# Chunked attention and a squared-ReLU FFN on one core: V of the first 512 tokens loaded in 1 KB packets and spread by TensorE

## The chip, the core and the metric

The kernel runs on one core of a Trainium2 chip. The metric is the device time of one execution in microseconds. Before the change three runs took 282.87, 282.85 and 281.72 us, so the median is 282.85 us. One further execution was taken by the hardware profiler. All trace times below are microseconds from the start of that execution's span.

## The reference

```python
# q, k, v: [8 batches, 8 heads, 576 tokens, 64], float32; attention inside chunks of 64 tokens
scores = matmul(q_c, k_c.T) / sqrt(64)           # per batch, head and chunk: 64 x 64
attn = exp(scores - max); attn = attn / sum(attn)
out = matmul(attn, v_c)
x = out.transpose(0, 2, 1, 3).reshape(4608, 512)  # tokens x (heads * 64)
h = maximum(x @ w_in, 0)                          # w_in 512 x 2048
y = (h * h) @ w_out                               # w_out 2048 x 512; y is 4608 x 512, float32
```

## The kernel before

The 4608 tokens are cut into 18 groups of 256, and two groups make a block of 512 tokens. For every block the kernel computes attention, then the first product of the FFN (`ffn_in`, matmuls at L479), then the second product. TensorE does the products of block j while the attention of later groups is put between them at slots that are written out by hand. The order of instructions on each engine is the order of the program text (`manual_schedule`), so a waiting instruction holds up everything behind it on its engine.

The first block has nothing in front of it. It has a path of its own, written at the end of the function, and this path is what the change touches. It works on halves of four heads (`u` = 0 and 1):

- `load_half` (L227) brings q and k of four heads and 512 tokens in one DMA on SP's queue. Four neighbouring tokens go to one partition, so the pieces are 1 KB long: partition p holds tokens 4p to 4p + 3. `load_v_half` (L236) brings V with one token to a partition in pieces of 256 B: four DMAs of 128 tokens for each half, into `v_first`, which lies in the buffer `w_sum` that is free until later. All these DMAs stand on SP's queue in the order q0, k0, q1, k1, eight of V, and then the weights (`load_w_in`, L162).
- `load_w_in(0, n_cast=2)` brings the first 256 of w_in's 2048 columns; POOL casts them to bf16 in two pieces (L165). One piece serves one `ft` of `ffn_in`.
- `transpose_half` (matmuls against the identity at L257, copies at L266) makes the transposed q and k of one half. For q the copy keeps the order of the PSUM bank; for k `by_token=True` puts the tokens back in order.
- `scores_half` (L278) makes the scores of one half, and ScalarE writes their exponentials `e` (L285).
- `values_half` (L298) multiplies `e` with V, which has a column of ones beside it; VectorE takes the reciprocal of that column (L305) and multiplies (L306).
- `transpose_x_half` (L314) transposes the result, and a copy (L318) puts it into `xT`. `ffn_in` reads `xT`: the steps `dt` = 0 and 1 read the heads of `u` = 0, the steps `dt` = 2 and 3 those of `u` = 1.
- `keep_busy(n)` (L325) is n matmuls of the identity whose result nobody reads.

`ps_ffn` is a ring of four PSUM banks, and `ps_att` a ring of two double banks. Each call takes the next buffer of its ring and waits until the last reader of that buffer is done. The opening ends with four steps of `ffn_in` for `ft` = 0 and 1 (those with `dt` = 0 and 1), the last `transpose_x_half` and its copy. From there on the main run of L479 goes through.

Of the kernel before, what the change touches and what calls it, by code (L numbers as in the profile page):

```python
# [10 lines left out]
FP32 = mybir.dt.float32  # L11
BF16 = mybir.dt.bfloat16
# [5 lines left out]
def kernel(  # L18
# [9 lines left out]
    nc = tc.nc  # L28

    B, H, S, D = q.shape  # L30
# [27 lines left out]
    const_pool = ctx.enter_context(tc.tile_pool(name="const", bufs=1))  # L58
# [5 lines left out]
    ps_ffn = ctx.enter_context(tc.tile_pool(name="ps_ffn", bufs=4, space=bass.MemoryType.PSUM))  # L64
# [6 lines left out]
    ident = const_pool.tile([128, 128], BF16, name="ident")  # L71
# [4 lines left out]
    w_sum = w_pool.tile([128, 3, n_ft // 2, d_model // 2], BF16, name="w_sum")  # L76
# [124 lines left out]
    def transpose_qk(g, q_pool, k_pool):  # L201
# [13 lines left out]
            transpose_paired(g, which, bank)  # L215
            copy_paired(copy, qkT[:, which], bank)

    v_first = w_sum.rearrange("p i f c -> p (i f c)")[:, 0:8 * H * (D + 1)].bitcast(
        FP32).rearrange("p (t h d) -> p t h d", t=4, h=H)
# [12 lines left out]

    def load_v_half(u):
        b, s = first
        for t in range(4):
            nc.sync.dma_start(  # L236
                out=v_first[:, t, 4 * u:4 * u + 4, 0:D],
                in_=v[b, 4 * u:4 * u + 4, s + 128 * t:s + 128 * t + 128, :].rearrange(
                    "h s d -> s h d"))

    def bank_bf16():
        return ps_ffn.tile([128, 512], FP32, name="ps_ffn").bitcast(BF16)

    def transpose_half(src, dst, copies, by_token=False):
        flat = dst.rearrange("c t h q -> c (t h q)")
        n = 1024 // len(copies)
        if len(copies) == 1:
            banks = [bank_bf16()] * 2
            at0 = (0, 512)
        else:  # L250
            banks = [bank_bf16(), bank_bf16()]
            at0 = (0, 0)
        for h in range(2):
            cols = banks[h][:, at0[h]:at0[h] + 512].rearrange("c (n i p) -> c i n p", n=8, i=4)
            for i in range(4):
                for a in range(2):
                    nc.tensor.transpose(  # L257
                        out=cols[64 * a:64 * a + 64, i],
                        in_=src[:, 2 * h + a, i, 1::2],
                        identity=ident)  # L260
        for i, copy in enumerate(copies):
            out_, in_ = flat[:, i * n:(i + 1) * n], banks[i][:, 0:n]
            if by_token:
                out_ = out_.rearrange("c (n p i) -> c n p i", n=8, i=4)
                in_ = in_.rearrange("c (n i p) -> c n p i", n=8, i=4)
            copy(out=out_, in_=in_)  # L266

    def scores_half(qkT):
        qT, kT = (qkT[:, w].rearrange("c t h q -> c (t h q)").rearrange(
            "c (h n q) -> c h n q", h=2, n=8) for w in range(2))  # L270
        ps = ps_att.tile([128, 1024], FP32, name="ps_att")
        for h in range(2):
            for t in range(4):
                for a in range(2):
                    for p in range(2):
                        rows = slice(64 * a, 64 * a + 64)
                        o0 = a * 512 + h * 256 + t * 64
                        nc.tensor.matmul(  # L278
                            out=ps[64 * p:64 * p + 64, o0:o0 + 64],
                            lhsT=kT[rows, h, 2 * t + p],  # L280
                            rhs=qT[rows, h, 2 * t + p],
                            start=True, stop=True)
        e = att_pool.tile([128, 2, n_hp, 2, 64], BF16, name="e")
        flat = e.rearrange("p a h t q -> p (a h t q)")
        nc.scalar.activation(  # L285
            out=flat.rearrange("p (b q i) -> p b q i", q=16, i=4),
            in_=ps.rearrange("p (b i q) -> p b q i", i=4, q=16), func=AF.Exp, scale=scale)
        return flat.rearrange("p (a h t q) -> p a h t q", a=2, h=2, t=4)

    def values_half(e, x, u, j):  # L290
        v_bf = v_first.bitcast(BF16)
        ps = ps_att.tile([128, 2, 512], FP32, name="ps_att")
        for t in range(2):
            for h in range(2):
                for a in range(2):
                    for p in range(2):
                        o0 = (2 * t + h) * (D + 1)
                        nc.tensor.matmul(  # L298
                            out=ps[64 * p:64 * p + 64, a, o0:o0 + D + 1],
                            lhsT=e[64 * p:64 * p + 64, a, h, 2 * j + t, :],  # L300
                            rhs=v_bf[64 * p:64 * p + 64, 2 * j + t, 4 * u + 2 * h + a, 1::2],
                            start=True, stop=True)
        o = ps[:, :, 0:4 * (D + 1)].rearrange("p a (h d) -> p a h d", d=D + 1)
        rec = att_pool.tile([128, 2, n_hp], FP32, name="rec", bufs=4)
        nc.vector.reciprocal(out=rec, in_=o[:, :, :, D])  # L305
        nc.vector.tensor_tensor(  # L306
            out=x[:, 4 * j:4 * j + 4].rearrange("p b a d -> p a b d"),
            in0=o[:, :, :, 0:D],
            in1=rec.to_broadcast([128, 2, n_hp, D]),
            op=ALU.mult)  # L310

    def transpose_x_half(x, u, j, copy, psb):
        for b in range(4):
            nc.tensor.transpose(  # L314
                out=psb[:, b * 128:(b + 1) * 128],
                in_=x[:, 4 * j + b].rearrange("p a d -> p (a d)"),
                identity=ident)
        copy(  # L318
            out=xTs[0][:, 2 * j:2 * j + 2, 2 * u:2 * u + 2, :],
            in_=psb[:, 0:512].rearrange("p (t h q) -> p t h q", t=2, h=2))  # L320

    def keep_busy(n):
        ps = ps_ffn.tile([128, 512], FP32, name="ps_ffn")
        for _ in range(n):
            nc.tensor.matmul(  # L325
                out=ps[:, 0:256], lhsT=ident, rhs=ident_f32.bitcast(BF16), start=True, stop=True)
# [151 lines left out]
    def ffn_in_step(h, xT, c, n, ft, dt):  # L478
        nc.tensor.matmul(  # L479
            out=h[:, 0:n],  # L480
            lhsT=w_in_bf[:, dt, ft * 128:(ft + 1) * 128],
            rhs=xT[:, c // 128:(c + n) // 128, dt, :],
            start=(dt == 0), stop=(dt == n_dt - 1))
# [170 lines left out]

    HT = BT // 2
    A, V = nc.scalar.copy, nc.vector.tensor_copy
    qh, kh = [], []
    for u in range(2):
        qh.append(load_half(q, u, "q_sb"))
        kh.append(load_half(k, u, "k_sb"))  # L660
    for u in range(2):
        load_v_half(u)
    load_w_in(0, n_cast=2)
    xTs[0] = att_pool.tile([128, BT // 128, n_dt, 128], BF16, name="xT", bufs=2)
    qkTs = [att_pool.tile([128, 2, 2, n_hp, 128], BF16, name="qkT", bufs=4) for _ in range(2)]
    xs = [att_pool.tile([128, 2, n_hp, 2, D], BF16, name="x", bufs=3).rearrange(
        "p t h a d -> p (t h) a d") for _ in range(2)]
# [1 line left out]
    keep_busy(12)  # L669
    transpose_half(qh[0], qkTs[0][:, 0], [V])  # L670
    keep_busy(3)
    transpose_half(kh[0], qkTs[0][:, 1], [V, A], by_token=True)
    keep_busy(3)
    e0 = scores_half(qkTs[0])
    transpose_half(qh[1], qkTs[1][:, 0], [V])
    keep_busy(2)
    transpose_half(kh[1], qkTs[1][:, 1], [V, A], by_token=True)
    keep_busy(4)
    e1 = scores_half(qkTs[1])
    keep_busy(6)  # L680
# [130 lines left out]
```

## Time and profile before

| | before |
|---|---|
| runs | 281.72, 282.85, 282.87 us; median 282.85 |
| the profiled execution | 281.53 us: a span of 279.8, and 1.73 around it |
| TensorE busy, 0 to 20 us | 16.17 us |
| TensorE busy, 20 to 276.3 us | 255.54 of 256.30 us |
| TensorE busy, 276.3 to the end | 0.00 of 3.50 us |
| first step of the main run of L479 | 19.93 us |

The profile has one row for a group of instructions. PE is TensorE's matmuls, PEld its weight loads, DVE is VectorE, ACT is ScalarE, POOL is GpSimd, and SP is the engine whose queue issues most DMAs. In the timeline, the columns are the start, the time from the first start to the last end, the engine, the line, the operation, output<-input, the shapes and the count; in brackets stand the engine's idle time before the group and what ended it. In the chain of work that ended last, each row is a start, a length, and the line that held the path. A matmul's row includes its way through the array, so that rows of neighbouring matmuls overlap. Some matmul records can be missing.

### The profile page before, as it was taken

The numbers are of one execution on the slowest core, as the hardware profiler recorded it, in microseconds if no ns is written. First come the engines' busy times: TensorE is split into PE (matmuls) and PEld (weight loads), VectorE is DVE, ScalarE is ACT, GpSimd is POOL, SyncE is SP. The second block draws the span as 40 slices with busy tenths as digits, with TensorE's granted clock in tenths as the row PEclk, the third lists the DMA queues.
The fourth block names the chain that finished last, engine by engine and source line by source line (L and its number), as shares of the span: only waits on it lengthen the run. The fifth ranks groups of instructions, "written<-read, shape, count | busy, mean of one in ns | idle before, by whom it ended". The sixth has DMA issues, their size and how long they took to land.

```text
span 279.8 us, 7189 instructions
## 1 busy us (share of the span) xinstructions
PE 271.7 (97%) x2968; PEld 178.0 (64%) x2968; DVE 187.2 (67%) x304; ACT 160.1 (57%) x269; POOL 36.0 (13%) x62
## 2 busy tenths in 40 slices
PE   6979999999999999999999999999999999999994
PEld 4634444788774487448844874487448744874584
DVE  0347505899953495579649954995579649955793
ACT  1437705786348853877197719762878197218710
POOL 2046733340370000000000000000000000000012
PEclk9999999999999999999999999999999999999999
DMA  7999999999999999998999999588789962241003
GB/s 228 224 340 358 365 330 245 321 226 222 240 219 245 229 216 174 262 236 173 216 284 242 188 262 235 121 160 158 202 228 207 221 203 40 39 108 45 0 20 132
DMA packets 144384, 57.09 MB, mean 204 GB/s; under 512 B 110624, under 2 KB 141600, under 8 KB 144352
## 3 DMA queue, kind: packets, MB, share of 16 engines
q1 hardware_dynamic: 143296, 53.62, 82.0%
q0 software_dynamic: 912, 2.88, 2.8%
q8 instruction: 23, 0.38, 0.6%
q10 hardware_dynamic: 144, 0.13, 0.1%
q14 instruction: 9, 0.07, 0.1%
HBM read 36.70 MB, written 9.44 MB: 165 GB/s over the span
## 4 chain that ended last, share of the span: by engine, by line
PE 83%; DVE 9%; ACT 3%; issue 2%; DMA 1%; ACTq 0%; DVEq 0%
PE ps_ffn L479 39%; PE ps_ffn L532 31%; PE ps_ffn L625 5%; DVE x L408 2%; DVE gT L474 2%; DVE w_st L492 2%; ACT rl L470 2%; PE ps_ffn L325 2%; DMA q_sb<-in_q_dram 1%; PE ps_att L400 1%; PE ps_ffn L257 1%; PE ps_att L373 1%; ACT e L384 1%; PE ps_att L427 1%; DVE rec L407 1%
## 5 line engine op out<-in xcount | busy, mean ns | idle before, releaser
L479 PE MATMUL ps_ffn<-xT,w_in_bf 128*128 128x512 bf16 (+1 forms) x640 | 130.1, 358 | 1.4 <-ACT xT L318 0.7
L474 DVE TENSOR_TENSOR gT<-rl 128x512 bf16<-128x512 f32 (+2 forms) x132 | 73.9, 592 | 59.6 <-ACT rl L470 58.9
L470 ACT ACTIVATE rl<-ps_ffn 128x512 f32<-128x512 f32 (+2 forms) x160 | 85.4, 553 | 27.4 <-PE ps_ffn L479 23.8
L479 PEld LDWEIGHTS <-w_in_bf 128*128 128x128 bf16 x640 | 60.6, 98 | 58.6 <-POOL w_in_bf L165 1.3
L532 PEld LDWEIGHTS <-w_st 128*128 128x128 bf16 x640 | 62.0, 98 | 8.1 <-DVE w_st L492 0.9
L492 DVE TENSOR_TENSOR w_st<-gT 128x2048 bf16<-128x2048 bf16 x40 | 47.3, 1219 | 0.2
L532 PE MATMUL ps_ffn<-w_out_bf,w_st 128*128 128x256 bf16 x384 | 45.1, 273 | 0.2
L532 PE MATMUL ps_ffn<-w_sum,w_st 128*128 128x256 bf16 x256 | 29.6, 273 | 0.0
L615 ACT COPY o_sb<-ps_ffn 128x512 f32<-128x512 f32 (+1 forms) x8 | 4.5, 560 | 41.1 <-PE ps_ffn L532 41.1
L532 PEld LDWEIGHTS <-gT 128*128 128x128 bf16 x256 | 24.8, 98 | 4.4 <-DVE gT L474 0.2
L567 POOL DMA_DIRECT2D out_dram<-o_sb x4 | 2.2, 553 | 187.3 <-DVE o_sb L492 187.3
L408 DVE TENSOR_TENSOR x<-ps_att,rec 128x512 bf16<-128x512 f32 x32 | 22.1, 692 | 1.1
L384 ACT ACTIVATE e<-ps_att 128x1024 bf16<-128x1024 f32 x16 | 15.8, 1021 | 4.8 <-PE ps_att L373 4.8
L472 ACT ACTIVATE gT<-rl 128x512 bf16<-128x512 f32 (+2 forms) x28 | 16.8, 599 | 0.9
L532 PE MATMUL ps_ffn<-w_out_bf,gT 128*128 128x256 bf16 x128 | 15.3, 273 | 0.0
L532 PE MATMUL ps_ffn<-w_sum,gT 128*128 128x256 bf16 x128 | 15.3, 273 | 0.0
L625 PE MATMUL ps_ffn<-w_out_bf,gT 128*128 128x512 bf16 x64 | 14.5, 380 | 0.0
L165 POOL CAST w_in_bf<-w_st 128x1024 bf16<-128x1024 f32 (+1 forms) x9 | 8.5, 949 | 18.4 <-DMA w_st<-in_moe_w_in_dram 18.4
L339 ACT CAST qkb<-k_sb 128x1024 bf16<-128x1024 f32 x10 | 10.5, 1047 | 0.1
L625 PEld LDWEIGHTS <-gT 128*128 128x128 bf16 x64 | 6.0, 98 | 7.0
L332 ACT CAST qkb<-q_sb 128x1024 bf16<-128x1024 f32 x10 | 10.4, 1045 | 0.0
L400 PEld LDWEIGHTS <-e 64*64 64x64 bf16 x512 | 5.7, 107 | 6.5 <-DVE x L408 2.1
(63 smaller groups left out, 163.1 us busy)
## 6 DMA issues: line engine op xcount, KB each, us to landing
q_sb<-in_q_dram SPq DMA_DIRECT2D x16, 512.0 KB, 5.8
k_sb<-in_k_dram SPq DMA_DIRECT2D x24, 256.0 KB, 6.1
out_dram<-o_sb SPq DMA_DIRECT2D x20, 256.0 KB, 3.4
w_st<-in_moe_w_in_dram SPq DMA_DIRECT2D x8, 512.0 KB, 6.6
w_st<-in_moe_w_out_dram SPq DMA_DIRECT2D x8, 512.0 KB, 6.2
ve_sb<-in_v_dram SPq DMA_DIRECT2D x28, 128.0 KB, 3.8
vo_sb<-in_v_dram SPq DMA_DIRECT2D x21, 128.0 KB, 3.2
out_dram<-o_sb POOLq DMA_DIRECT2D x9, 256.0 KB, 5.2
```

Of the source, the lines that this page charges most:

```text
L165: nc.gpsimd.tensor_copy(out=w_in_bf[:, :, i * 256 + c:i * 256 + c + n], in_=st[:, :, c:c + n])
L332: copy(out=qkb[:, 0].rearrange("p (i h d) -> p i h d", i=2, h=H), in_=qk[g][0].rearrange("p t h d -> p (t h d)").rearrange("p (h i d) -> p ...
L339: copy(out=state["qkb", g][:, 1], in_=qk[g][1].rearrange("p t h d -> p (t h d)"))
L384: nc.scalar.activation(out=e_out, in_=s_in, func=AF.Exp, scale=scale)
L408: nc.vector.tensor_tensor(out=x[:, t].rearrange("p h a d -> p a h d"), in0=o[:, :, :, 0:D], in1=rec.to_broadcast([128, 2, n_hp, D]), op=AL ...
L470: nc.scalar.activation(out=rl[:, 0:n], in_=h[:, 0:n], func=AF.Relu)
L472: nc.scalar.activation(out=gT[:, ft, c:c + n], in_=rl[:, 0:n], func=AF.Square)
L474: nc.vector.tensor_tensor(out=gT[:, ft, c:c + n], in0=rl[:, 0:n], in1=rl[:, 0:n], op=ALU.mult)
L479: nc.tensor.matmul(out=h[:, 0:n], lhsT=w_in_bf[:, dt, ft * 128:(ft + 1) * 128], rhs=xT[:, c // 128:(c + n) // 128, dt, :], start=(dt == 0) ...
L492: engine.tensor_tensor(out=out, in0=in0, in1=in1, op=op)
L532: nc.tensor.matmul(out=outs[t], lhsT=a[:, i, t * 128:(t + 1) * 128], rhs=b[:, i, :], start=(first and i == 0 and (last or t == 0)), stop=( ...
L625: nc.tensor.matmul(out=o_ps[tt], lhsT=gT[:, ft, tt * 128:(tt + 1) * 128], rhs=w_out_bf[:, ft, :], start=(ft == 0), stop=(ft == n_ft - 1))
```

## The change

V of the first block is loaded like q and k: one DMA for each half, four tokens to a partition, 1 KB pieces (`load_half(v, u, ...)`, into buffers of the q and k pools). `load_v_half` is gone. SP's queue now has q0, k0, v0, q1, k1, v1 and then the weights.

To put each token on its own partition, POOL makes a matrix `spread` of zeros and ones, and `spread_v` runs 32 matmuls for each half: for even and odd heads (`a`), four token places `i` and four row groups `t` of 32 partitions, a matmul with 32 rows, 128 columns of weights and 2 x 64 moving columns. The four `t` write four PSUM banks, that is all of `ps_ffn`. Four copies (128x256) then write `v_first`, which is now bf16 and dense.

`transpose_half` loses `by_token`: k keeps the order of the bank, as q does. `scores_half` and `values_half` swap the halves of the partitions for odd heads (`c = p ^ a`). The copy of q1 goes from VectorE to ScalarE. TensorE's opening is put in another order, and 16 of the 40 `keep_busy` matmuls go.

```diff
+    spread = const_pool.tile([128, 240], BF16, name="spread")
+    nc.gpsimd.memset(spread, 0.0)
+    for t in range(4):
+        rows = slice(32 * t, 32 * t + 32)
+        nc.gpsimd.tensor_copy(out=spread[rows, 48:176]..., in_=ident[rows, 32 * t:32 * t + 32]...)
+        nc.gpsimd.tensor_copy(out=spread[rows, 176:192], in_=ident[rows, 32 * t:32 * t + 16])
...
-    def load_v_half(u):
-        b, s = first
-        for t in range(4):
-            nc.sync.dma_start(
-                out=v_first[:, t, 4 * u:4 * u + 4, 0:D],
-                in_=v[b, 4 * u:4 * u + 4, s + 128 * t:s + 128 * t + 128, :].rearrange(
-                    "h s d -> s h d"))
...
+    def spread_v(src, u, copies):
+        outs = [ps_ffn.tile([128, 512], FP32, name="ps_ffn") for _ in range(4)]
+        for a in range(2):
+            for i in range(4):
+                c0 = 48 + 64 * a - 16 * i
+                for t in range(4):
+                    rows = slice(32 * t, 32 * t + 32)
+                    nc.tensor.matmul(
+                        out=outs[t][:, 0:256].rearrange("p (h a d) -> p h a d", h=2, a=2)[:, :, a],
+                        lhsT=spread[rows, c0:c0 + 128],
+                        rhs=src[rows, a::2, i, 1::2],
+                        start=(i == 0), stop=(i == 3))
+        for t, copy in enumerate(copies):
+            copy(
+                out=v_first[:, t, 4 * u:4 * u + 4, 0:D],
+                in_=outs[t][:, 0:256].rearrange("p (h d) -> p h d", h=4))
...
     for u in range(2):
         qh.append(load_half(q, u, "q_sb"))
         kh.append(load_half(k, u, "k_sb"))
-    for u in range(2):
-        load_v_half(u)
+        vh.append(load_half(v, u, ("q_sb", "k_sb")[u]))
     load_w_in(0, n_cast=2)
...
     keep_busy(12)
     transpose_half(qh[0], qkTs[0][:, 0], [V])
     keep_busy(3)
-    transpose_half(kh[0], qkTs[0][:, 1], [V, A], by_token=True)
+    transpose_half(kh[0], qkTs[0][:, 1], [V, A])
     keep_busy(3)
     e0 = scores_half(qkTs[0])
-    transpose_half(qh[1], qkTs[1][:, 0], [V])
+    spread_v(vh[0], 0, [V, V, V, A])
+    transpose_half(qh[1], qkTs[1][:, 0], [A])
+    values_half(e0, xs[0], 0, 0)
+    transpose_half(kh[1], qkTs[1][:, 1], [V, A])
+    values_half(e0, xs[0], 0, 1)
     keep_busy(2)
-    transpose_half(kh[1], qkTs[1][:, 1], [V, A], by_token=True)
-    keep_busy(4)
     e1 = scores_half(qkTs[1])
-    keep_busy(6)
-    values_half(e0, xs[0], 0, 0)
-    values_half(e0, xs[0], 0, 1)
-    keep_busy(4)
+    spread_v(vh[1], 1, [V, V, A, A])
     transpose_x_half(xs[0], 0, 0, A, bank_bf16())
-    keep_busy(4)
     transpose_x_half(xs[0], 0, 1, A, bank_bf16())
     values_half(e1, xs[1], 1, 0)
     values_half(e1, xs[1], 1, 1)
-    keep_busy(2)
-    xb = [bank_bf16(), bank_bf16()]
+    xb = [ps_ffn.tile([128, 512], FP32, name="ps_ffn") for _ in range(2)]
     begun = {ft: ps_ffn.tile([128, 512], FP32, name="ps_ffn") for ft in range(2)}
-    transpose_x_half(xs[1], 1, 0, A, xb[0])
+    keep_busy(4, xb[1])
+    transpose_x_half(xs[1], 1, 0, A, xb[0].bitcast(BF16))
     for ft in range(2):
         for dt in range(n_dt // 2):
             ffn_in_step(begun[ft], xTs[0], 0, BT, ft, dt)
-    transpose_x_half(xs[1], 1, 1, V, xb[1])
+        if ft == 0:
+            transpose_x_half(xs[1], 1, 1, V, xb[1].bitcast(BF16))
```

More of the change, by code (lines that the diff above doesn't have):

```diff
@@ L216, in transpose_qk @@
             copy_paired(copy, qkT[:, which], bank)
-    v_first = w_sum.rearrange("p i f c -> p (i f c)")[:, 0:8 * H * (D + 1)].bitcast(
-        FP32).rearrange("p (t h d) -> p t h d", t=4, h=H)
+    spread = const_pool.tile([128, 240], BF16, name="spread")
+    nc.gpsimd.memset(spread, 0.0)
+    for t in range(4):
+        rows = slice(32 * t, 32 * t + 32)
+        nc.gpsimd.tensor_copy(
+            out=spread[rows, 48:176].rearrange("p (b x) -> p b x", b=2)[:, :, 0:16],
+            in_=ident[rows, 32 * t:32 * t + 32].rearrange("p (b x) -> p b x", b=2))
+        nc.gpsimd.tensor_copy(out=spread[rows, 176:192], in_=ident[rows, 32 * t:32 * t + 16])
+    v_first = w_sum.rearrange("p i f c -> p (i f c)")[:, 0:4 * H * (D + 1)].rearrange(
+        "p (t h d) -> p t h d", t=4, h=H)
     nc.gpsimd.memset(v_first[:, :, :, D:D + 1], 1.0)
@@ L231, in load_half, with transpose_half @@
             "p (h i d) -> p h i d", h=4, i=4)
-    def load_v_half(u):
-        b, s = first
-        for t in range(4):
-            nc.sync.dma_start(
-                out=v_first[:, t, 4 * u:4 * u + 4, 0:D],
-                in_=v[b, 4 * u:4 * u + 4, s + 128 * t:s + 128 * t + 128, :].rearrange(
-                    "h s d -> s h d"))
     def bank_bf16():
         return ps_ffn.tile([128, 512], FP32, name="ps_ffn").bitcast(BF16)
-    def transpose_half(src, dst, copies, by_token=False):
+    def transpose_half(src, dst, copies):
         flat = dst.rearrange("c t h q -> c (t h q)")
@@ L261, in transpose_half @@
         for i, copy in enumerate(copies):
[L262 to L266, printed above, removed]
+            copy(out=flat[:, i * n:(i + 1) * n], in_=banks[i][:, 0:n])
     def scores_half(qkT):
@@ L275, in scores_half @@
                     for p in range(2):
+                        c = p ^ a
                         rows = slice(64 * a, 64 * a + 64)
@@ L278, in scores_half @@
                         nc.tensor.matmul(
-                            out=ps[64 * p:64 * p + 64, o0:o0 + 64],
+                            out=ps[64 * c:64 * c + 64, o0:o0 + 64],
                             lhsT=kT[rows, h, 2 * t + p],
@@ L288, in scores_half @@
         return flat.rearrange("p (a h t q) -> p a h t q", a=2, h=2, t=4)
+    def spread_v(src, u, copies):
[14 more added lines that the diff above has]
+                in_=outs[t][:, 0:256].rearrange("p (h d) -> p h d", h=4))
     def values_half(e, x, u, j):
-        v_bf = v_first.bitcast(BF16)
         ps = ps_att.tile([128, 2, 512], FP32, name="ps_att")
@@ L296, in values_half @@
                     for p in range(2):
+                        c = p ^ a
                         o0 = (2 * t + h) * (D + 1)
@@ L299, in values_half @@
                             out=ps[64 * p:64 * p + 64, a, o0:o0 + D + 1],
-                            lhsT=e[64 * p:64 * p + 64, a, h, 2 * j + t, :],
-                            rhs=v_bf[64 * p:64 * p + 64, 2 * j + t, 4 * u + 2 * h + a, 1::2],
+                            lhsT=e[64 * c:64 * c + 64, a, h, 2 * j + t, :],
+                            rhs=v_first[64 * c:64 * c + 64, 2 * j + t, 4 * u + 2 * h + a, :],
                             start=True, stop=True)
@@ L320, in transpose_x_half, with keep_busy @@
             in_=psb[:, 0:512].rearrange("p (t h q) -> p t h q", t=2, h=2))
-    def keep_busy(n):
-        ps = ps_ffn.tile([128, 512], FP32, name="ps_ffn")
+    def keep_busy(n, ps=None):
+        if ps is None:
+            ps = ps_ffn.tile([128, 512], FP32, name="ps_ffn")
         for _ in range(n):
@@ L656 @@
     A, V = nc.scalar.copy, nc.vector.tensor_copy
-    qh, kh = [], []
+    qh, kh, vh = [], [], []
     for u in range(2):
```

## The prediction

> **What bounds the kernel now.** I read the page first, then the busy time in three stretches, to find where time can be won at all.
>
> ```profile
> span 279.8 us, 7189 instructions
> PE 271.7 (97%) x2968; PEld 178.0 (64%) x2968; DVE 187.2 (67%) x304; ACT 160.1 (57%) x269; POOL 36.0 (13%) x62
> ```
>
> The second line gives busy time by engine: TensorE is the bound. By stretches it is busy for 16.17 of the first 20 us, for 255.54 of the 256.30 us that follow, and not at all in the last 3.5. So from 20 us on it has 0.76 us of idle time in all, and whatever moves the first step of the main run of L479 moves the end by as much. That step starts at 19.93. The timeline of the opening, the rows that decide it:
>
> ```profile
> 2.89 9.55 SPq L236 DMA_DIRECT2D w_sum<-in_v_dram  x8
> 12.48 7.68 SPq L162 DMA_DIRECT2D w_st<-in_moe_w_in_dram  x7
> 15.97 0.21 DVE L305 RECIPROCAL rec<-ps_att 128x8 f32<-128x8 f32 x1 [0.88 <-PE ps_att L298]
> 17.36 1.17 POOL L165 CAST w_in_bf<-w_st 128x512 bf16<-128x512 f32 x2 [15.09 <-DMA w_st<-in_moe_w_in_dram]
> 18.02 1.16 PE L479 MATMUL ps_ffn<-xT,w_in_bf 128*128 128x512 bf16 x4 [0.66 <-ACT xT L318]
> 19.02 0.39 PE L314 MATMUL ps_ffn<-ident,x 128*128 128x128 bf16 x4
> 19.45 0.42 DVE L318 COPY xT<-ps_ffn 128x512 bf16<-128x512 bf16 x1 [1.70 <-PE ps_ffn L314]
> ```
>
> Eight V issues keep SP's queue for 9.55 us, 1.2 each, so the first weights are issued at 12.48. They land at 17.30, the two casts end at 17.97 and 18.52, and the four early steps of L479 can only go then. Behind them in TensorE's order stands the last x transpose, although its input was ready at 17.74 (17.05 and 0.69 of L306). The chain of waits, in order of time, names ScalarE's copy for 18.02, which ends within 0.02 us of the first cast; the second pair of steps waits for the second cast alone.
>
> ```profile
> 5.97 0.75 PE ps_ffn L325 x3
> ...
> 12.13 0.76 PE ps_ffn L325 x6
> ...
> 17.39 0.59 ACT xT L318
> ...
> 19.18 0.24 PE ps_ffn L314 x4
> 19.42 0.02 issue
> 19.45 0.44 DVE xT L318
> 19.88 0.05 issue
> 19.93 13.12 PE ps_ffn L479 x60
> ```
>
> The first two rows are a second thing to see: three fillers took as long at 6 us as six did at 12 us. TensorE runs at half rate until 10.4 us, and the page's clock row (9 in every slice) does not show it.
>
> **The change, part by part.**
>
> *Loads.* SP's issues of 1 KB pieces take 0.5 us each (q0 at 0.73, k0 at 1.25), so six of them end near 4 us and the weights follow at once. From then on the transfer counts, not the issue: with 1 KB pieces the weights land 1.5 us apart (17.30, 18.67, 20.17; later 23.50, 25.00, 26.50). q0 and k0 land at 4.86 and 6.29 as now; then v0 at 7.8, q1 at 9.3 (now 8.29), k1 at 10.8 (now 9.90), v1 at 12.3 (the last V lands at 15.87 now), the first weights at 13.8 instead of 17.30. The casts end at 15.0. Every later load comes earlier by up to 3.5 us, and POOL's casts behind it too.
>
> *POOL.* A memset and eight small copies come behind the memsets that end at 2.27. The nearest rows are 0.10 (memset, L85) and 0.29 (cast of 128x128, L72): 0.9 to 2.6 us, so `spread` is ready between 3.2 and 4.9 and is first needed at 9.1. Four microseconds of waiting for q0, k0 and their scores cover it. It stands behind the cast of the identity, so the first fillers still start at 1.71.
>
> *The 32 matmuls of a half.* Before has no 32-row tile. At full rate a 128-column matmul alone takes 56 ns (L314: four in 0.39, of which 0.22 is the way out of the last). Score matmuls use 64x64 tiles in four corners of the array: 32 of them in 0.45, so 8.2 ns each where 64 columns alone take 28, that is over three at a time. If four row groups overlap like this, 32 spread matmuls take 32 x 14 = 0.45 us at full rate and 0.9 at half rate. If they don't overlap, 32 x 56 = 1.8 us, and 3.4 at half rate. I take the overlap: the score row is the nearest, with the same mixing of weight loads and matmuls. The Trainium skill (TensorE: Matmul & The Clock Gate, section LDWEIGHTS) speaks against it: a load of 32 rows costs as much as one of 128 rows, about 107 ns for 128 columns. By it, if the loads went in single file, a spread would take 3.4 us; the L314 row disagrees for full tiles, at 56 ns a matmul with its load.
>
> *Copies.* A 128x256 copy out of a bank took 0.425 on VectorE and 0.373 on ScalarE (both L615); two such on VectorE follow each other after 0.34 (two of L492 in 0.77). k's copy in bank order should cost 0.42 like L318 instead of 0.69. q1's copy costs 1.01 on ScalarE (L432) instead of 0.69 on VectorE.
>
> *The new path.* Until the first scores nothing moves: L278 from 8.40, exponentials from 9.10 to 10.12. Then, with the row lengths above:
> - Spread 0 starts at 9.15, still at half rate, and is out at 10.3. Its banks were freed by k0's copies at 8.35. VectorE's three copies end at 10.67, 11.02 and 11.36.
> - A new wait: q1's transposes need the first spread bank, so TensorE, with everything behind them, stands from 10.0 to 10.72. Then 0.64 (the L257 row at 10.48): out at 11.36. ScalarE's copy ends at 12.41.
> - First values at 11.24, out at 11.55; reciprocal and multiply take 0.93 (15.97 to 16.90 now), to 12.50. k1's transposes run from 11.43 to 12.07; k1's copies stand behind the multiply on VectorE and behind q1's on ScalarE, and end at 12.84 and 12.90.
> - Second scores from 12.95 to 13.39 (now from 11.69). So this wait costs 1.26 here. Exponentials until 14.44.
> - Spread 1 from 13.27, out at 13.93. VectorE's copies end at 14.33 and 14.68, ScalarE's, behind the exponentials, at 14.71 and 14.99.
> - The second half's values are behind the x transposes and that last copy: from 15.05 to 15.50, where they now end at 15.95 and 16.23. The cover of the fillers is gone here and nothing fills it, but the path gets 0.5 shorter.
> - Two reciprocals and multiplies take 1.77 (15.97 to 17.74 now): 15.39 to 17.16. The early steps of L479 have their weights since 15.0 and go beside this.
> - The last x transpose from 17.2 to 17.6, its copy to 18.04, the main run from 18.09.
>
> So the gain is 19.93 - 18.09 = 1.84 us: about 0.5 from values that come earlier, the rest because the last x transpose no longer stands behind steps that wait for weights. What is late next is not a load but the copies between the four banks. The six loads have room: in this sum they could come 1.7 us apart without moving 18.09.
>
> **The numbers against the runs.** The profiled execution took 281.53 (279.8 and 1.73 around it): 279.7 after. The runs' median is 1.3 above it, which gives 281.0. I do not know which of the two a run of the new kernel is like, and forecast the middle, 280.4.
>
> **Rivals.**
> 1. *The clock.* The new order leaves TensorE idle from 10.0 to 10.7 and takes fillers out. If the full rate comes only after the second scores, two transposes of 0.43 more each and the values move the main run to 19.06 (gain 0.87: 280.7, or 282.0 by the median). If it comes after 17 us, all later groups double too: 20.20, 0.27 slower than now. For it: an idle stretch of 0.46 stands at 4.45 and full rate came 6 us after that. Against it: the spread is real multiplication where now a transpose stands. The Trainium skill (the same page, Parts 1 and 4) gives windows of about 3.4 us and says that transposes don't count as busy; by it a switch missed at 10.4 comes at 13.8, which is the 0.87 case. No row here shows the window.
> 2. *Slower: the row groups don't overlap.* TensorE then has 1.8 instead of 0.45 us in each spread, the first one partly at half rate. Place: between first scores and q1's transposes, and between second scores and x transposes. Price: the main run starts at 20.45, 0.52 late: 282.05, or 283.4 by the median, and up to 21.8 (283.4, 284.7) with a late clock. It decides above 46 ns for a spread matmul at full rate; at 28 the gain is still 1.06.
> 3. *It doesn't do what it says:* the six loads don't land sooner, since the stream and not the packet size is the limit. At 2.0 us a load the main run starts at 19.64, gain 0.3: 281.2, or 282.5. Against it: between 12 and 13 us now the DMA engines are busy for 0.45 of their time and move 100 GB/s, so the queue is starved there.
>
> Against a gain that is given back later speak the 0.76 us of idle time after 20 us.
>
> **How the numbers follow.** Overlap and clock as now: 0.50. Rival 1: 0.25, rival 2: 0.17, rival 3: 0.08. A measurement here can tell about 0.5%, or 1.41 us, from no change, so faster means below 281.44 and slower above 284.26. The forecast case lies nearly all below 281.44 (0.48), of rival 1 two fifths (0.10): 0.58 faster. Slower are the late clock with single file (0.08) and a little of rival 1 (0.02): 0.10. The rest, 0.32, is the same. The range begins at 279.0, since a clock that switches at 8 us would bring the main run to 17.3, and reaches to 283.0, which takes in rival 1 at both bases and half of rival 2.
>
> **What would show it.** Right: spread groups of about 0.9 (first) and 0.45 us (second); w_in's first cast near 13.8; a TensorE gap of 0.5 to 0.7 ahead of q1's transposes; second scores near 13; the main run of L479's successor (L495) at 18.1. Wrong: fillers or transposes at half rate after 11 us, spread groups over 1.5 us, or a main run that starts on time but stops later.

## The result, and the profile after

| | before | after |
|---|---|---|
| median of the runs beside each other | 282.19 us (10 runs) | 284.88 us (10 runs) |
| ratio | | 1.0114, 95% interval 1.0086 to 1.0141 |
| the profiled execution | 281.53 us | 287.61 us, the slowest of the ten |

The change makes the kernel slower by 1.1%. Medians are over all executions, while the ratios leave out those that fell into a slower state.

The profiled execution is the worst of the ten. Four at a mean granted clock of 0.992 to 0.994 took 283.97 to 284.34 us, two at 0.988 took 285.12 and 285.33, two at 0.982 took 285.94 and 286.01, and the profiled one had 0.976. The one at 1.000 took 284.63, still 2.4 above the median of before, so the clock is not all of the loss.

The page of the profile after, cut to four of its rows (span, engines, clock in tenths by slice, the queue that carries nearly all DMAs):

```profile
span 285.8 us, 7298 instructions
...
PE 273.7 (96%) x3016; PEld 179.5 (63%) x3016; DVE 189.6 (66%) x308; ACT 162.7 (57%) x273; POOL 38.4 (13%) x71
...
PEclk9658999999999999999999999999999999999999
...
q1 hardware_dynamic: 140128, 53.62, 84.3%
```

Before, the clock row had a 9 in every slice. Now slices 2 to 4 (7 to 29 us) have 6, 5 and 8. The busy time in three stretches:

```profile
0.00:20.00 20.00, 14.74 (x290) 10.42 (x291) 6.17 (x16) 7.61 (x11) 6.58 (x37) 0.73 0.94 306
20.00:22.94 2.94, 2.94 (x14) 1.51 (x13) 1.05 (x2) 0.59 (x1) 2.08 (x2) 0.50 0.96 320
22.94:282.30 259.36, 255.88 (x2716) 167.54 (x2714) 181.94 (x290) 154.49 (x261) 29.69 (x32) 1.00 0.88 191
```

After the stretch and its length comes TensorE's busy time; the number ahead of the last two is its granted clock. In the third row it stands for 259.36 - 255.88 = 3.48 us; before it stood for 0.76 between 20 and 276.3 us. So the time went to two places, and the opening is only one of them. TensorE's timeline of the opening:

```profile
7.16 0.64 PE L276 MATMUL ps_att<-qkT 64*64 64x64 bf16 x32
9.80 1.04 PE L295 MATMUL ps_ffn<-q_sb,spread 32*128 32x128 bf16 x32 [2.00 <-DMA q_sb<-in_v_dram]
11.40 1.06 PE L258 MATMUL ps_ffn<-ident,q_sb 128*64 128x128 bf16 x16 [0.56 <-DVE w_sum L301]
...
14.71 0.64 PE L276 MATMUL ps_att<-qkT 64*64 64x64 bf16 x32
15.29 0.50 PE L295 MATMUL ps_ffn<-k_sb,spread 32*128 32x128 bf16 x11
16.18 0.81 PE L295 MATMUL ps_ffn<-k_sb,spread 32*128 32x128 bf16 x21 [0.39 <-issue]
17.42 1.01 PE L329 MATMUL ps_ffn<-ident,x 128*128 128x128 bf16 x8 [0.42 <-DVE w_sum L301]
...
21.10 0.63 PE L329 MATMUL ps_ffn<-ident,x 128*128 128x128 bf16 x4
21.52 4.75 PE L495 MATMUL ps_ffn<-xT,w_in_bf 128*128 128x512 bf16 x18
```

TensorE stood for V for 2.00 us, for the first bank for 0.56, and for its own instructions ("issue") for 0.39. It went to half rate at 9.29, by the trace's clock records, and stayed there until 22.94. The fifth step of `ffn_in`, the first of the main run, came at 19.93 before and comes at 22.38 here, 2.45 us later; the half rate, which lasts two steps more, makes it 2.7. Some 3.5 us more are lost far from the change, matched matmul by matmul: 0.65 at 61 us (x transposes wait for VectorE), 1.7 at 79 to 82 us, and 1.3 at 228 to 233 us, where TensorE waits for xT and qkT, which come by transposing DMAs.

### The profile page after: what moved, and what is told of

Read it like the earlier page. It is cut to its first block, busy times and chain, and to the rows that moved or that the text cites. A ratio compares the mean times of both kernels' runs of the same rounds, so it can differ in the third digit from the quotient of the medians.

```text
span 285.8 us, 7298 instructions
## 1 busy us (share of the span) xinstructions
PE 273.7 (96%) x3016; PEld 179.5 (63%) x3016; DVE 189.6 (66%) x308; ACT 162.7 (57%) x273; POOL 38.4 (13%) x71
## 3 DMA queue, kind: packets, MB, share of 16 engines
q1 hardware_dynamic: 140128, 53.62, 84.3%
## 5 line engine op out<-in xcount | busy, mean ns | idle before, releaser
L508 DVE TENSOR_TENSOR w_st<-gT 128x2048 bf16<-128x2048 bf16 x40 | 49.0, 1261 | 0.2
```

The lines of the kernel that those rows point to most:

```text
L508: engine.tensor_tensor(out=out, in0=in0, in1=in1, op=op)
```

## The experiments

All ratios are to runs of the kernel before on the same chip in the same series. "The opening" is the lead or lag of the matched matmul of the main run at 20.4 us. The first four runs ask what happens in the opening.

### The change again (e1, control), and without the wait for V (e3)

e1 is the change unaltered; e3 differs in one word, so that the first spread reads k's half, which has landed by then. The values of half the first block's heads are then made from k.

```diff
-    spread_v(vh[0], 0, [V, V, V, A])
+    spread_v(kh[0], 0, [V, V, V, A])
```

> The changed kernel, unaltered, as a control and for a second profile. Theory A (the stretch in which TensorE stands for V's first half lets its clock fall to half rate, in the trace from 9.29 to 22.94 us): the clock differs from run to run, and the time with it, about 0.85 us for each 3.4 us at half rate; 284 to 286 us. Theory B (V's first half lands late, at 9.76 instead of 7.8, because some DMA engines lag): V lands late again in this profile. Theory C (the stalls after 23 us, 3.5 us longer than before, are a lasting part of the loss): they are there again, with over 2 us.

> The first spread reads k's first half, which has landed, instead of V's: TensorE does not wait for V's load there (so half of the heads of the first 512 tokens get other values; V is loaded all the same). Theory B (the late landing is what makes TensorE stand): the first spread starts near 7.9, the clock stays, the main run starts near 18 to 19, and the time is 2.5 to 3.5 us under the control's. Theory A alone agrees. If the path through banks and copies is the cause: under 1 us better than the control.

The control: 284.42 us, ratio 1.0101 (1.0055 to 1.0146). In its trace V's first half landed at 9.40, TensorE stood for it for 0.98 us, the clock was at half rate from 10.77 to 21.01, and the opening lagged by 1.92. Without the wait: 284.12 us, 1.0072 (1.0040 to 1.0104). The clock was full from 6.8 us to the end, and the opening led by 0.94 instead of lagging, so in this execution the wait is what let the clock fall. It is not the only thing that can: of e3's 12 executions three have a mean granted clock of 1.000, and of the 16 of the change and its control one. What TensorE still stood for, in the main:

```profile
9.83 0.64 PE L258 MATMUL ps_ffn<-ident,q_sb 128*64 128x128 bf16 x16 [1.05 <-DMA q_sb<-in_q_dram]
...
11.34 0.64 PE L258 MATMUL ps_ffn<-ident,k_sb 128*64 128x128 bf16 x16 [0.62 <-DMA k_sb<-in_k_dram]
...
14.35 0.51 PE L295 MATMUL ps_ffn<-k_sb,spread 32*128 32x128 bf16 x21 [1.10 <-issue]
```

But with an opening better by nearly 3 us than the control's, the run won only 0.3 us: its span had lost 4.5 us against the kernel before by the end, of which 3.6 between 216 and 226 us.

### Fillers in the waits (e2)

18 `keep_busy` matmuls where TensorE stood: 10 ahead of the first spread, and 4 ahead of two transposes, on banks that the next matmuls overwrite.

```diff
-    spread_v(vh[0], 0, [V, V, V, A])
+    spread_v(vh[0], 0, [V, V, V, A], fill=10)
+    pv = ps_att.tile([128, 2, 512], FP32, name="ps_att")
+    keep_busy(4, pv[:, 0])
...
-    values_half(e0, xs[0], 0, 0)
+    values_half(e0, xs[0], 0, 0, pv)
```

> 18 keep_busy matmuls are added where TensorE stands in the changed kernel: 10 ahead of the first spread, 4 behind it, 4 behind the second. Nothing else moves. Theory A (clock): no half rate after the first full-rate stretch, the main run of the first product starts near 20 instead of 22, and the time is 1.5 to 2.5 us under the control's. Theory B (V lands late): the wait stays, only the clock part comes back, under 1 us. A third theory (the spread, its copies and bank waits make the path itself longer than before): the same time as the control with a clock of 1.0.

285.61 us, ratio 1.0121 (1.0079 to 1.0164): no better. Yet the mechanism did what was asked: clock full from 5.8 us on, opening 0.77 ahead of the kernel before. The span was 2.6 longer all the same. TensorE's timeline around the largest late loss, and ScalarE's ahead of it:

```profile
213.28 3.67 PE L551 MATMUL ps_ffn<-w_out_bf,w_st 128*128 128x256 bf16 x32
218.66 3.65 PE L551 MATMUL ps_ffn<-w_sum,w_st 128*128 128x256 bf16 x32 [1.72 <-ACT n L607]
```

```profile
214.64 1.04 ACT L351 CAST qkb<-q_sb 128x1024 bf16<-128x1024 f32 x1 [0.76 <-DMA q_sb<-in_q_dram]
217.08 1.04 ACT L358 CAST qkb<-k_sb 128x1024 bf16<-128x1024 f32 x1 [1.39 <-DMA k_sb<-in_k_dram]
218.03 0.58 ACT L607 COPY n<-ps_ffn 128x512 f32<-128x512 f32 x1
```

ScalarE waits for the loads of q and k, and the copy that TensorE needs is queued behind the two casts. In the kernel before, the casts and the same copy ran without a wait:

```profile
213.16 1.05 ACT L332 CAST qkb<-q_sb 128x1024 bf16<-128x1024 f32 x1
214.29 1.05 ACT L339 CAST qkb<-k_sb 128x1024 bf16<-128x1024 f32 x1
215.46 0.59 ACT L588 COPY n<-ps_ffn 128x512 f32<-128x512 f32 x1
```

The two loads of q were also issued later, at 206.07 and 208.25 on SP's queue against 202.02 and 205.80 before. So the gain of the opening was given back because loads came late 200 us on. These loads were requested for later groups and have nothing to do with the opening's data.

### The old order of loads and products (e4)

V behind q1 and k1 on the queue; both halves' scores first, then the two spreads with their values. The edit of the loads:

```diff
     for u in range(2):
         qh.append(load_half(q, u, "q_sb"))
         kh.append(load_half(k, u, "k_sb"))
+    for u in range(2):
         vh.append(load_half(v, u, ("q_sb", "k_sb")[u]))
```

> The 1 KB loads and the spread stay, but the queue has q0, k0, q1, k1, v0, v1, and TensorE does both halves' scores first, then spread 0, values 0, spread 1, values 1. Theory A and B: TensorE has work while V is under way, the clock stays, the main run starts near 19, and the time is near 281, 1 us under before. If the spread and its copies are the cost: over before's 282.2 again.

284.86 us, 1.0116 (1.0072 to 1.0160). The opening lagged by 1.35 (half rate from 14.54 to 21.37), and the late losses came as in the control. So the order of the opening alone is not what the 1.1% hang on.

### Where the buffers stand (e5 to e8)

All four kernels lose 1.7 to 3.9 us at 214 to 232 us, with different openings. What they share: `spread` takes 480 bytes of each partition, and the pools behind it are moved by that. By the sizes of the tiles, before, the buffers of q, k, xT, qkT and x began on multiples of 128 bytes; after, 32 bytes short of one. The second candidate was that V's halves shift the ring of q's and k's buffers. Four kernels: `spread` in 512 bytes; the same with the fillers; the kernel before with 480 unused bytes; and the fillers with V in a part of `w_out_bf` that is still free, which leaves the ring as it was.

```diff
# e5 (and e6, with the fillers)
-    spread = const_pool.tile([128, 240], BF16, name="spread")
+    spread = const_pool.tile([128, 256], BF16, name="spread")
# e7, on the kernel before, with a memset of 16 columns by GpSimd
+    shift = const_pool.tile([128, 240], BF16, name="shift")
# e8, with the fillers
-        vh.append(load_half(v, u, ("q_sb", "k_sb")[u]))
+        vh.append(load_v_half(u))    # into w_out_bf[:, 8 + 4 * u:12 + 4 * u]
```

> The kernel after, with its constant matrix in 512 bytes of each partition instead of 480 (16 unused columns). The 480 bytes had moved every later buffer (the loads' targets, the weights' stages, qkT, xT) from multiples of 128 bytes to 32 bytes short of one; with 512 bytes they stand as in the kernel before. Address theory (transfers into buffers 32 bytes off take longer, so the loads run late and the kernel loses 2 to 3.5 us at 140 to 230 us): packets of 256 bytes return from a mean of 22.0 to 23.0 ns to about 21.0, and the time falls by 2 to 3 us to about 282; what is left of the loss lies in the opening, where the clock still halves. Buffer theory (the V halves shift the ring of load buffers): no change, 284.4. Phase theory (any shift of the opening makes the loads meet the transposes at worse moments): no change, 284.4, within 0.5.

> The fillers of e2 and the 512 bytes of e5 together. Address theory: the opening ends some 0.8 us earlier than in the kernel before, as in e2, and the late stand at 217 us is gone: about 281, a ratio of 0.995 to 1.0. Buffer theory and phase theory: as e2, 285, with the late stand of 1.7 us in its place.

> The kernel before with nothing changed but 480 unused bytes of each partition behind its constants (and a small memset of them by GpSimd), so that its buffers stand where those of the kernel after stand. Address theory: slower by 2 to 3 us, 284 to 285, with the stands at 140 to 230 us that all versions of the change had, and the 256-byte packets at 22 ns or more. Buffer theory and phase theory: no change, ratio 1.0 within 0.3 per cent.

> e2 (fillers, 480 bytes) with V's halves loaded into a part of w_out_bf that is still unused then, so that the ring of q_sb and k_sb goes on as in the kernel before. Buffer theory: the late stand is gone, about 281 to 282. Address theory and phase theory: as e2, 285 within 0.8.

| spread's bytes | without fillers | with fillers |
|---|---|---|
| 480 | 1.0101 (1.0055 to 1.0146) | 1.0121 (1.0079 to 1.0164); own V buffers: 1.0105 (1.0072 to 1.0138) |
| 512 | 1.0062 (1.0024 to 1.0101) | 1.0019 (0.9983 to 1.0055) |

The kernel before with 480 unused bytes: 287.52 us, ratio 1.0132 (1.0076 to 1.0188). It has none of the change, and it loses no less than the change does, at the same place and by the same wait as e2:

```profile
214.18 3.67 PE L534 MATMUL ps_ffn<-w_out_bf,w_st 128*128 128x256 bf16 x32
219.92 3.65 PE L534 MATMUL ps_ffn<-w_sum,w_st 128*128 128x256 bf16 x32 [2.07 <-ACT n L590]
```

So the late loss comes with the 480 bytes, not with V or its spread; the ring is out as a cause, since V in its own buffers changes nothing. With the fillers the step from 480 to 512 bytes is clear of the noise; without them it is not, and the 284.78 us of e5 are not the 282 expected. The fillers are worth nothing at 480 bytes and 2 us at 512 by the medians (284.78 against 282.73; 1.2 us by the ratios, whose intervals overlap). That fits e2's trace: as long as late loads decide, an earlier opening is only waited away. The profiled execution of the 512 bytes with fillers took 280.66 us, 0.9 less than that of the kernel before; its median is not distinguishable from before's.

### Which addresses (e9 to e17)

Two more shifts of the kernel before (64 and 128 bytes in place of 480, everything else the same), a shift of 32 bytes behind q's and k's buffers only, and 640 bytes for the version with fillers.

```diff
-    shift = const_pool.tile([128, 240], BF16, name="shift")
+    shift = const_pool.tile([128, 32], BF16, name="shift")    # e9; 64 columns in e10
# e11: 16 columns, in a pool of its own between q's and k's buffers and qkT
# e12: e6 with spread = const_pool.tile([128, 320], ...)
```

> The kernel before with 64 unused bytes of each partition behind its constants where e7 had 480 (the same memset). Buffers keep multiples of 64 bytes. If only the 32 bytes off a multiple of 64 cost the 3.7 us of e7: no change against the kernel before, ratio 1.0 within 0.3 per cent, and 256-byte packets at 21.0 ns. If the loads need multiples of 128: about as slow as e7, 285 to 287. If it were not the address but the memset or anything else that e7 added: as slow as e7.

> The same with 128 bytes: the load buffers, which start 384 bytes beyond a multiple of 512 in the kernel before, start on a multiple of 512. If 64 is the limit: no change. If a larger multiple helps as well: 256-byte packets below 21 ns and a time of 280 to 281.5, below the kernel before.

> The kernel before with 32 unused bytes behind the load buffers of q and k: the weights' stages, q_sb, k_sb and V's buffers stay where they are, and qkb, qkT, xT, x, gT and the output buffers move by 32 bytes, as in e7. If the loads of q and k into their buffers are what the 32 bytes slow: no change, 282. If it is the transposes and the stores, which read and write the moved buffers: slower by 2 to 4 us, 284 to 286.

> e6 (fillers) with the constant matrix in 640 bytes, so that the load buffers start on multiples of 512. If only multiples of 64 matter: as e6, 282.7 within 0.8. If 512 helps: 280 to 281.5, faster than the kernel before. In both cases TensorE still stands about 1 us after its 223rd matmul, where every version of the change stood for its next block of instructions (0.39 to 1.28 us).

64 bytes: 1.0165 (1.0115 to 1.0216). 128 bytes: 1.0030 (0.9996 to 1.0063). 32 bytes behind the load buffers: 1.0153 (1.0102 to 1.0203). 640 bytes with fillers: 283.32 us, 1.0043 (1.0014 to 1.0072). With 64 bytes every buffer stays on a multiple of 64, and the kernel still lost. Larger multiples than 128 won nothing.

Then one group of buffers at a time by 32 bytes, the others by 0 or 128, and as a control both unused tiles of e15 at 128 bytes:

```diff
# e13: q_sb, k_sb        e14: gT, rl, o_sb, n
# e15: qkb and rec       e16: xT, qkT, x, e
# e17: as e15, with 128 bytes in both places
+    moved = att_pool.tile([128, 64], BF16, name="moved", bufs=1)
+    nc.gpsimd.memset(moved, 0.0)
```

> The kernel before with q_sb and k_sb alone moved by 32 bytes (all behind them by 128). e11 moved everything but these and lost 4.3 us, so if the cause is the same for all, here little is left: 282 to 283.2, as e10 (all by 128). If the loads of q and k suffer as well: 284 or more.

> Only gT, rl, o_sb and the n buffers moved by 32 bytes: the stores read from them, no transposing transfer does. If the transposing transfers are the cause: 282 to 283.2. If the stores are: 284.5 to 287.

> Only qkb (and the small rec) moved by 32 bytes, the source of the 14 transposing transfers into qkT; the feed-forward buffers by 128. If the source counts: 284 to 287. If the target counts, or the stores: 282 to 283.2.

> Only xT, qkT, x and e moved by 32 bytes, that is, the targets of all 26 transposing transfers and the source of the 12 into xT; the rest by 128 or not at all. If the targets of the transposing transfers count: 284 to 287. If the source qkb or the stores: 282 to 283.2.

> e15 with 128 bytes in both places where it had 32 and 96: same instructions, same number of tiles, all buffers of q, k, x and of the transposing transfers on multiples of 128. If the 32 bytes are the cause: 282 to 283.2. If the second unused tile or its memset is: 287 to 289, as e15.

| run | moved by a step off 128 | ratio | queue q1's time |
|---|---|---|---|
| before | none | | 229.4 us |
| e10 | none | 1.0030 | 221.1 |
| e14 | feed-forward and output buffers (32) | 1.0009 (0.9984 to 1.0033) | 232.3 |
| e7 | all (480) | 1.0132 | 238.9 |
| e9 | all (64) | 1.0165 | 241.8 |
| e11 | all behind q_sb, k_sb (32) | 1.0153 | 238.5 |
| e13 | q_sb, k_sb (32); two unused tiles | 1.0184 (1.0144 to 1.0225) | 239.8 |
| e15 | qkb, rec (32); two unused tiles | 1.0218 (1.0188 to 1.0247) | 237.0 |
| e16 | xT, qkT, x, e (32); two unused tiles | 1.0209 (1.0169 to 1.0249) | 236.8 |
| e17 | none; two unused tiles | 1.0176 (1.0124 to 1.0227) | 238.0 |

The last column is the share of q1 in the page times the span of that one profile, that is, how long the same 53.62 MB kept the DMA engines. It parts the kernels of the table cleanly: 221 to 232 us in those that lose at most 0.3%, 236 or more in the others (the change itself: 84.3% of 285.8 is 240.9; with 512 bytes and fillers 229.8). A packet of 256 bytes took 20.2 to 21.3 ns in the mean in the first, 22.0 to 22.8 in the others. It does not tell what one execution loses: the profiled one of e10, at 286.71 us the longest of its 12, has the shortest queue time of all and still lost 4 us between 225 and 235 us, 2.33 of them in one wait for qkT. Nor does the opening part the kernels: the main run began at 19.95 in e13, which lost, and at 18.62 in e12, which lost only 0.4%.

What is shown: e7, e9, e10, e11 and e14 run the same instructions in the same order and differ only in addresses, and three of them lose 1.3 to 1.7% while two do not. What is not: a rule. "Multiples of 128" fits these five only if the feed-forward and output buffers of e14 do not count, and it fits the versions with 480, 512 and 640 bytes; but the control e17 keeps all multiples of 128 and loses 1.76%. With it, e13, e15 and e16 say nothing on which buffer it is, since two unused tiles go with the loss even where no buffer leaves its multiple of 128. The control lost like the others, by a wait of the same kind:

```profile
130.26 3.67 PE L535 MATMUL ps_ffn<-w_out_bf,w_st 128*128 128x256 bf16 x32
136.37 3.81 PE L535 MATMUL ps_ffn<-w_sum,w_st 128*128 128x256 bf16 x20 [2.44 <-ACT n L591]
```

Whether distances between buffers count, or how the loads meet the transposing transfers in time, stays open. The Trainium skill (DMA: Bandwidth & Descriptors, How a descriptor splits into AXI transactions) says that a read which starts off a multiple of 256 bytes costs extra 32-byte beats. By the sizes of the tiles, q_sb and k_sb start 128 bytes beyond such a multiple in the kernel before, 96 in e7 and 0 in e10; by my estimate from the page a row of 256 bytes there takes 12, 11 and 8 beats. The loads write these buffers, which the page does not speak of, and the runs do not follow this order: e7 is slower than before and e10 is not faster.

### An earlier V and earlier weights without the change (e18)

The kernel before, with V's second half issued by GpSimd, so that SyncE reaches the weights sooner.

```diff
-            nc.sync.dma_start(
+            (nc.sync, nc.gpsimd)[u].dma_start(
                 out=v_first[:, t, 4 * u:4 * u + 4, 0:D],
```

> The kernel before with the four transfers of V's second half issued by GpSimd instead of SyncE. SyncE is then through with V at about 7.7 us instead of 12.43 and issues the first weights 4.7 us sooner; they should land at 13 to 14 instead of 17.30, and V complete before 14 instead of 15.87. The last x transposes still stand behind the early steps, which no longer wait for weights. Sum: values of the second half from 15.1, x at 17.0, the last copy at 17.9, main run from about 18.3 to 18.7 instead of 19.93: 280.3 to 280.8, ratio 0.994 to 0.997. Rival: GpSimd's issues are slow (over 2 us each) and V's second half comes later than now: 282 to 284.

283.93 us, 1.0060 (1.0032 to 1.0088): a miss, and not by the rival that I had named. GpSimd issued its four in 3.1 us. But k's second half landed at 11.95, two microseconds later than before, TensorE stood for it for 2.67 us, and the clock was at half rate from 12.55 to 15.96:

```profile
11.99 0.64 PE L257 MATMUL ps_ffn<-ident,k_sb 128*64 128x128 bf16 x16 [2.67 <-DMA k_sb<-in_k_dram]
```

No version was shown to beat the kernel before.

## Why the prediction was wrong

I forecast 280.4 us and a gain of 1.84; it is a loss of 2.7 by the medians. By its steps:

*The base: right reading, one execution.* In all ten traces of the old opening (before, e7, e9 to e11, e13 to e17) the main run begins 2.6 us after the first weights land, as the prediction read it. But that landing varies, from 15.88 to 17.33, and the main run begins at 18.51 to 19.95. The rows of e11, an early one:

```profile
15.93 1.17 POOL L167 CAST w_in_bf<-w_st 128x512 bf16<-128x512 f32 x2 [13.61 <-DMA w_st<-in_moe_w_in_dram]
16.60 1.16 PE L482 MATMUL ps_ffn<-xT,w_in_bf 128*128 128x512 bf16 x4
```

The 19.93 of the forecast is at the late end. With the clock held, the change's main run begins at 18.62 to 19.65 (e2, e3, e6, e8, e12), within the same span. Of the kernels that lose at most 0.4%, those with the old opening begin at 19.65 to 19.93 (before, e10, e14) and those with the new one at 18.62 and 18.87 (e12, e6): a gain of 0.8 to 1.3, in few traces. At 480 bytes e7 begins at 19.18 and the change with the clock held at 18.99 to 19.65: no gain.

*Loads: the size was off.* v0 was to land at 7.8. In the trace 14 of its 16 completion marks come by 7.46, and the last two, of two DMA engines, at 9.73 and 9.76. The lag stays: q1 11.27, k1 12.77, v1 14.28, first weights 15.75, each 2.0 later than forecast, 1.5 apart as forecast. It changes from run to run: v0 landed at 9.40 in the control, 8.28 in e3, 7.58 in e2. "The six loads have room" was wrong by more than the lag: v0 had none. "Until the first scores nothing moves" put their end near 9.1; they ended at 7.80, so that v0 would have come just in time even at 7.8. Full rate came at 5.88 instead of 10.39, and in every trace here other than before's it came between 4.41 and 7.74.

*Clock: the deciding term in the opening, given 0.25 and the wrong price.* Rival 1 had it at 0.97 to 2.1 us against the forecast; the main run came 4.29 late (22.38 instead of 18.09). After standing for 2.0 us came four half-rate stretches in a row: 13.65 us, four times 3.41. The length of a stand does not set their number: after 2.67 us in e18 came one, after 0.98 and 0.87 in the control three. The Trainium skill (TensorE: Matmul & The Clock Gate, Part 1) gives a window of 3.413 us, and the records agree in every run where the rate fell before the end (for 3.41, 6.83, 10.24 or 13.65). The same page asks for a whole idle window before the rate falls; the trace shows less to be enough: in the window from 5.88 to 9.29, after which the rate fell, TensorE ran matmuls until 7.80. With the clock held, the opening led that of before's one trace by 0.28 to 1.30 (e2, e3, e6, e8, e12).

*A stand that the sum did not have.* In all nine traces of the change and its versions TensorE stops after its 223rd matmul, for 0.39 to 1.28 us, "issue" in the profile, whichever product stands there: the spread's 11th in the change, the scores' 29th with fillers.

```profile
12.32 0.44 PE L276 MATMUL ps_att<-qkT 64*64 64x64 bf16 x29
13.83 0.22 PE L276 MATMUL ps_att<-qkT 64*64 64x64 bf16 x3 [1.07 <-issue]
...
17.96 0.40 PE L332 MATMUL ps_ffn<-ident,x 128*128 128x128 bf16 x4
18.19 6.04 PE L498 MATMUL ps_ffn<-xT,w_in_bf 128*128 128x512 bf16 x26
```

These are 512 bytes with fillers. The instruction queue of the trace moves blocks of 16 KB; here one starts at 11.27 and takes 1.13, and TensorE goes on 1.4 later; in all nine it goes on 1.2 to 1.5 after the block's end. That it waits for this block is argued from these times. In the kernel before the same block came at 10.20, and the 223rd matmul at 15.77, so nothing stood. Why the block is later now (11.3 to 13.8) was not tried. Apart from this, the sum of the new path holds in this trace: at 14.07 the second spread is 0.80 late against the forecast, and the main run begins, with the fifth step, at 18.87 instead of 18.09, 0.78 late (18.19 is the third and fourth early step, which stand behind the last transposes).

*"Against a gain that is given back later speak the 0.76 us of idle time."* This is the step that failed most. 0.76 us of idle time shows that nothing held TensorE up in that execution; it doesn't show how near the loads were to doing so. The page of before has a 9 in the DMA row (engines busy for 90% or more) in nearly every slice from 7 to 175 us and again from 210 to 224, and with the loads a little slower such a queue gave back e2's lead and more: 1.72 at 217 us. And the constant of 480 bytes, of which I noted only that POOL makes it in time, was a costly part of the diff: 480 unused bytes make the old kernel slower by 1.3%, and 512 instead of 480 with the fillers bring the new one from 1.0121 to 1.0019. Why these bytes cost time stays open.

*What held.* `spread` was ready at 3.95 (forecast 3.2 to 4.9). The row groups overlap: 32 matmuls in 1.04 us at half rate and 0.64 at full rate, four starting together every 107 ns at half rate, so rival 2 was rightly put low; single file would have been 3.4 by the forecast's estimate. The copies took 0.42 to 0.43 on VectorE, 0.34 apart, and 0.374 on ScalarE. The casts of the first weights ended at 16.98 and held up nothing.

## What to carry to other kernels

An engine that is busy for 99.7% of a stretch does not prove that a lead will be kept: look at the DMA rows too, and where they are full, ask which loads have room. Before costing a new tile at nothing, ask where it puts all the tiles behind it; a variant of the old kernel with only an unused tile of that size shows in one run whether its place costs anything, though e17 shows that such a tile needs a control of its own. Before forecasting from one trace, ask how far its starting point moves from execution to execution. In an opening, a wait of a microsecond or two was not priced here by its length but by the clock stretches that followed; cheap matmuls in the waits kept the clock in e2, e6, e8 and e12.

## What the runs showed of the hardware that I had not expected

- Unused bytes ahead of the buffers change the time of a kernel with otherwise equal instructions (1.0165 of the time before with 64 bytes in e9, 1.0030 with 128 in e10), and the DMA queue's time with it (241.8 against 221.1 us).
- One or two of a load's 16 completion marks came 0.7 to 2.3 us after the others in the third load of the change's kernel (after, e1, e3, e5), and the next loads kept the lag.
- VectorE's 128x2048 bf16 product took 2.05 us instead of 1.22 where casts of GpSimd ran beside it. The two rows of GpSimd, and the range of the product in the same kernel (minimum, median, maximum in ns):

```profile
75.33 1.13 POOL L348 CAST qkb<-q_sb 128x1024 bf16<-128x1024 f32 x1 [12.64 <-DMA q_sb<-in_q_dram]
77.17 1.26 POOL L355 CAST qkb<-k_sb 128x1024 bf16<-128x1024 f32 x1 [0.72 <-DMA k_sb<-in_k_dram]
```

```profile
L508 DVE TENSOR_TENSOR w_st<-gT x40: 1215/1219/2056, 70.8 to 277.6; 128x2048 bf16<-128x2048 bf16 x40
```

Two of the 40 were long, at 75.5 and 77.5 us, each begun 0.15 to 0.28 us after a cast had begun; this is the 1.7 us at 79 to 82 us in the change's profile. In e2 it was the other way round: the product began at 73.1, a cast 0.2 later, and the cast took 1.94 us while all 40 products stayed at 1.22. Which of the two began first depended on when a load landed.
